# Attention in front of a soft mixture of experts: rotary products, sums and roundings placed earlier, the row of maxima on another queue

## Chip, cores and metric

The kernel runs on one core of a Trainium2 chip. The metric is the device time of one execution in microseconds (us), lower is better. Engines are named as in the profile: PE (matrix products), PEld (its weight loads), DVE (vector), ACT (scalar/activation), POOL (GpSimd) and SP (SyncE, which here only issues DMAs). A "q" behind a name (ACTq, SPq) is that engine's sequencer, for instance while it issues a DMA.

## What is computed

The reference is an attention, a soft mixture of experts on its output, and a gated MLP on that. Only the attention part is touched by the change:

```python
def rotate(x):
    x1, x2 = (x[..., :half], x[..., half:])
    return np.concatenate([x1 * cos - x2 * sin, x1 * sin + x2 * cos], axis=-1)
q_rot, k_rot = (rotate(q), rotate(k))
scores = scale * np.matmul(q_rot, k_rot.transpose(0, 1, 3, 2))
scores = scores - np.max(scores, axis=-1, keepdims=True)
attn = np.exp(scores)
attn = attn / (np.sum(attn, axis=-1, keepdims=True) + 1e-09)
return np.matmul(attn, v)
```

There are 4 batches of 8 heads, 576 positions, head size 64. Then `x` is [2304, 512]; `_moe_ref` (8 experts, 4 slots each, 512 to 1024 to 512) and `_moe2_ref` (512 to 2048 to 512 with `h * sigmoid(h)`) follow.

## The kernel before

**Pairs and groups.** The 32 heads are worked on as 16 pairs `p` of two heads. The attention of one pair is ten groups: two halves `h` of the 576 queries, and in each half five chunks `c` of keys in the order 4, 0, 1, 2, 3, where chunk 4 holds the remaining 64 keys of both heads together. `groups` (160 entries) is the order of PE's main work, and the loop over `g` near the end of the attention code writes everything out by hand: nothing is scheduled by a planner. In each turn it emits `scores` (four matmuls and two exponentials; chunk 4 has four matmuls and one), at most one unit of the row maxima, `esum`, `session`, and then `run(g)`, the list of further tasks that stand under this group's number. Below, "place i" is g modulo 10, so places 0 and 5 are the chunk 4 groups.

**Exponentials.** `scores` makes two products for each tile of scores (L397 and L398, for chunk 4 L386 and L387): one of the rounded keys and queries, and one with 65 rows, of which the last is a row of -1 on the key side and the row of maxima on the query side (row 64 of the tile `qb`). ACT takes the exponential (L399, L388). Three buffers of PSUM (`st`) hold the scores.

**Row maxima.** A pair needs nine units. A unit is two products (L345; the first from `kd`, a difference of two halves of the keys made by `k_diff`, L334), a ReLU on ACT (L350) and a reduction on DVE (L359) that frees the second buffer. Three buffers of PSUM (`mx`) and two of SBUF hold them. `MAX_AT` says at which places of a pair's ten groups one unit is done: in the kernel before, at all but place 4. They serve the pair after next or the next one, since they start at place 6 (`MAX_FROM`). `max_rows` (L367) then transposes the nine columns of maxima on PE, and `max_copy` (L372) copies the result on ACT and issues the DMA into row 64 of `qb` (L373) from ACT's own queue. Both stand under `MAX_ROW`, four groups ahead of the pair's first group, that is at place 6.

**Rotary.** `rotary(p)` gives the steps for pair `p`; queries and keys lie in the tile `raw`, [128, 2 heads, 2, 576]. f0 (L269, DVE) multiplies by the cosine, f1 (L272, POOL) by the sine, f2 (L275, DVE) adds the two, f3 (L279, ACT) rounds the sum, f4 (L284, DVE) takes what the rounding left. Each is done once for each head, f0(0), f0(1) and so on. m0 and m1 (L288) are five DMAs on SP's queue that spread the result into `sa` and `kb`, m2 (L304) another one into `qb`. The tuples `ROT_2`, `ROT_3`, `ROT_4` (pairs 2, 3, 4) and `ROT` (pairs 5 to 15) give, for begin, f0(0), f1(0), f1(1), f0(1), f2(0), f2(1), f3(0), f3(1), m0, f4(0), f4(1), m1 in this order, how many groups ahead of the pair's first group each stands. -22 is thus place 8 of a pair's ten groups, two to three pairs earlier.

**The other tasks.** `load` (L224) fetches `raw` of a pair from HBM, at `QK_LOAD`; there are two buffers. `load_v` (L232) fetches the values. `fetch` (L138), `conv` (L148 on ACT, L151 and L154 on DVE) and `keep` (L647, L648) bring weights of the last stage to 32 bits; `W_IN_AT` places them. `load_w` (L134) prefetches weights of the experts. All of these DMAs are issued by SP, which works through its list in order and waits at each one until its buffer is free. `esum` (L411, L413, L414, L416) sums exponentials on POOL at places 2, 3, 7 and 8. `sums` (L435, L437, at places 2 and 7), `recip` (L440, L444) and `norm`, `norm2` (L448, L449, L455) make the quotient; `x_t` (L467, L471 to L477, at `X_T`) transposes the output; `batch` (`BATCH`) makes the mixture's logits and slots once for four pairs. `sums`, `x_t`, `max_rows` and parts of `batch` share one buffer of PSUM, with the tag `m`.

```python
ROT = (-29, -26, -27, -26, -25, -24, -22, -23, -22, -21, -21, -20, -20)
...
at(g0 + o[min(p, 5) - 2], rt(p, k, *a))
...
at(g0 + (MAX_ROW_1, MAX_ROW_2, MAX_ROW_3, MAX_ROW)[min(p, 4) - 1], lambda p=p: max_rows(p), lambda p=p: max_copy(p))
```

Of the kernel before, what the change touches and what calls it, by code (L numbers as in the profile page):

```python
# [7 lines left out]
F32 = mybir.dt.float32  # L8
# [9 lines left out]
NPAIR = 16  # L18
# [20 lines left out]
ROT_2 = (-26, -22, -19, -21, -23, -19, -19, -18, -18, -18, -17, -18, -17)  # L39
ROT_3 = (-31, -25, -27, -26, -26, -24, -23, -23, -22, -16, -22, -19, -15)  # L40
ROT_4 = (-28, -28, -26, -28, -24, -23, -23, -20, -22, -17, -19, -21, -17)
ROT = (-29, -26, -27, -26, -25, -24, -22, -23, -22, -21, -21, -20, -20)
Q_COPY = -6
V_LOAD = -6
K_DIFF_2 = -14
K_DIFF_3 = -15
K_DIFF_4 = -16
K_DIFF = -17
QK_LOAD = -34
QK_LOAD_3 = -54  # L50
QK_LOAD_4 = -31
MAX_ROW = -4
MAX_ROW_1 = -4
MAX_ROW_2 = -4
MAX_ROW_3 = -5
RECIP = 7
NORM = 7
X_T = ((21, 25), (15, 21), (15, 21), (15, 21))
W_IN_AT = (9, 20, 30, 40, 49, 60, 70, 81, 89, 100, 110, 120)
W_IN_STEPS = (1, 1, 5)  # L60
FETCH_AHEAD = 5
BATCH = (14, 16, 20, 21, 22, 23, 25, 30)
W_LOADS = (34, 54, 64, 75, 66, 84, 86, 76, 105, 95, 116, 135, 126, 144, 127, 134, 135, 136, 144, 155)
SCALES = -19
EARLY = -10
MAX_AT = (1, 1, 1, 1, 0, 1, 1, 1, 1, 1)
MAX_FROM = (6, 2, 6)
MAX_COUNTS = (0, 1, 2, 2, 2, 2, 0, 0, 1, 1, 1, 1, 1, 2, 2, 0, 1, 1, 1, 1, 1, 1, 1, 1, 1, 2, 1, 1, 1, 1, 1, 1, 1, 1, 2, 1, 1, 1, 1, 1)

# [5 lines left out]
def attn_softmoe_mlp_kernel(ctx: ExitStack, tc: tile.TileContext, qk, v, cst, phi, w1, w2, w_in, w_out, out):  # L75
    nc = tc.nc
    pe, act, dve, pool, sp = nc.tensor, nc.scalar, nc.vector, nc.gpsimd, nc.sync
# [113 lines left out]
    with tc.manual_schedule():  # L191
        with ExitStack() as t1:
# [22 lines left out]
            def operands(p):  # L215
                return sa[p % 3] + [qb_[p % 2], kb_[p % 3]]
# [3 lines left out]
            def load(p, heads=None, parts=(slice(0, 2),)):  # L220
                if p not in raw:
                    raw[p] = rw.tile([128, 2, 2, S], F32, tag=f"raw{p % 2}", name=f"raw{p}")
                if heads is None:
                    sp.dma_start(out=raw[p], in_=qk[p])  # L224
                else:
                    for hd in heads:
                        for i in parts:
                            sp.dma_start(out=raw[p][:, hd, i], in_=qk[p, :, hd, i])
# [135 lines left out]
            def max_rows(p):  # L364
                assert mdone[p] == 9
                t = ps_m.tile([128, 512], F32, tag="m", name=f"psm{p}")
                pe.transpose(t[0:9, 0:128], mx.pop(p), ident)  # L367
                mrow[p] = t

            def max_copy(p):  # L370
                m = (p2 if p % 2 else eb).tile([9, 128], F32R, tag="m", bufs=1, name=f"m{p}")
                act.activation(out=m, in_=mrow.pop(p)[0:9, 0:128], func=ACTF.Copy)  # L372
                act.dma_start(out=operands(p)[2][64:65].bitcast(F32), in_=m.bitcast(F32))  # L373

            et = {}
            u_ps = {}
# [82 lines left out]
            def x_t(p, part):  # L459
                b, j = divmod(p, 4)  # L460
                if j == 0 and part == 0:
                    xc[b] = p1.tile([128, 6, DM], F32, tag="x", name=f"x{b}")
                cs = [(c, n) for c, (o, n) in enumerate(CHUNKS[b]) if (o >= HS if b == 3 else c == 4) == part]
                t = ps_m.tile([128, 4, 128], F32, tag="m", name=f"xps{p}_{part}")
                for i, (c, n) in enumerate(cs):
                    o = CHUNKS[b][c][0]
                    pe.transpose(t[0:n, i], xt[p][:, o:o + n], ident)  # L467
                full = sum(n == 128 for c, n in cs)
                c0 = cs[0][0]
                if b == 3:  # L470
                    act.activation(out=xc[b][0:96, c0:c0 + 3, 128 * j:128 * j + 128], in_=t[0:96, 0:3], func=ACTF.Copy)  # L471
                    return
                if full:
                    act.activation(out=xc[b][:, c0:c0 + full, 128 * j:128 * j + 128], in_=t[:, 0:full], func=ACTF.Copy)
                if full < len(cs):
                    c, n = cs[-1]
                    act.activation(out=xc[b][0:n, c, 128 * j:128 * j + 128], in_=t[0:n, full], func=ACTF.Copy)  # L477
# [151 lines left out]
            def at(g, *fs):  # L629
                tasks.setdefault(g, []).extend(fs)  # L630
# [10 lines left out]
            def conv(i):  # L641
                n, k = divmod(i, 4)
                o = wa.tile([128, 512], F32, tag=f"w{NWA - 5 + i % 2}", name=f"w_in_32_{i}")

                def keep():
                    if n == 0:
                        sp.dma_start(out=w_in_0[:, k], in_=o[:, 0:128])  # L647
                    sp.dma_start(out=w_in_32[n][:, k], in_=o if n else o[:, 128:512])  # L648

                cv[i] = (*narrow(words.pop(i), o, wa, f"hw{i}", f"w{NWA - 3}"), keep)  # L650
# [11 lines left out]
            def begin_batch(b):  # L662
                bt[b] = batch(b)

            def bf(b, k, *a):
                return lambda: bt[b][k](*a)

            ROTARY = [([r[i] for r in (ROT_2, ROT_3, ROT_4, ROT)], k, a) for i, (k, a) in enumerate(((8, ()), (0, (0,)), (1, (0,)), (1, (1,)), (0, (1,)), (2, (0,)), (2, (1,)), (3, (0, act)), (3, (1, act)), (5, ()), (4, (0,)), (4, (1,)), (6, ())))]

            for p in range(NPAIR):  # L670
# [8 lines left out]
                if p >= 3:  # L679
                    at(g0 + (QK_LOAD_3, QK_LOAD_4, QK_LOAD)[min(p, 5) - 3], lambda p=p: load(p))  # L680
                if p >= 1:
                    at(g0 + (MAX_ROW_1, MAX_ROW_2, MAX_ROW_3, MAX_ROW)[min(p, 4) - 1], lambda p=p: max_rows(p), lambda p=p: max_copy(p))
                if p == NPAIR - 1:
# [8 lines left out]
                for i in range(2 * (p < NPAIR - 1)):  # L692
                    at(g0 + X_T[p % 4][i], lambda p=p, i=i: x_t(p, i))
                if p % 4 == 3 and p < NPAIR - 1:
                    b = p // 4
                    at(g0 + BATCH[0], lambda b=b: begin_batch(b), bf(b, 0, 0))
                    at(g0 + BATCH[1], bf(b, 0, 1))
                    at(g0 + BATCH[2], bf(b, 1, 0))
                    at(g0 + BATCH[3], bf(b, 1, 1))
                    at(g0 + BATCH[4], bf(b, 2))  # L700
                    at(g0 + BATCH[5], bf(b, 3))
                    at(g0 + BATCH[6], bf(b, 4))
                    at(g0 + BATCH[7], bf(b, 5))
            for i in range(12):
                gc = W_IN_AT[i]
                at(gc, lambda i=i: conv(i), lambda i=i: cv[i][0]())
# [79 lines left out]
            g3(0, act)  # L786
            nk(0)
            max_copy(0)
            h3q(0)
            load(2, (1,))  # L790
# [19 lines left out]
            for g in range(NG + 2):  # L810
                i = g % 10
                if g < NG:
                    p, h, c = groups[g]
                    if i == (MAX_FROM[p] if p < 3 else 6) and p + 2 < NPAIR:
                        ms += [(p + 2, u) for u in range(9)]
                    u = [ms.pop(0) for _ in range(min(len(ms), MAX_COUNTS[g] if g < len(MAX_COUNTS) else MAX_AT[g % 10]))]
                    way = [x[1] % 2 if g < 5 else 0 for x in u]
# [397 lines left out]
```

## Time and profile before

| what | value |
|---|---|
| median of 3 runs | 675.57 us (671.97 to 676.7) |
| the profiled execution's own time | 679.32 us |
| its span, first to last instruction | 677.5 us |
| mean granted TensorE clock | 0.959 of full speed |
| PE busy | 612.3 us, 90% of the span |
| DVE, ACT, POOL busy | 60%, 53%, 34% |

The profile is of one execution. Busy time of PE is modelled from pipelined matmuls, whose durations overlap; the start times tell how fast they follow each other. The attention lasts until about 390 us of the span; behind it come the experts (to about 430 us) and the gated MLP. A row that ends in "[1.54 <-DVE raw L275]" says that the engine stood idle for 1.54 us before this instruction and which instruction ended the wait.

### The profile page before, as it was taken

The page shows a single profiled execution, that of the slowest core. Times are in us where ns is not written, and L with a number is a line of the kernel's source. Part 1 is how long each engine was busy: PE and PEld are TensorE (multiplying, and loading weights), DVE is VectorE, ACT ScalarE, POOL GpSimd, SP SyncE. Part 2 cuts the span into 40 slices and gives each one's busy share as a digit, 9 for nine tenths or more (in the row PEclk, how much of TensorE's full clock was granted, in tenths as well). Part 3 has the DMA queues.
Part 4 walks back from the last instruction along what each step waited for, and adds up shares of the span by engine and source line. Part 5 has one row for each costly group of instructions (what it writes and reads, how often), then busy time and mean ns, then how long its engine had stood idle before and what let it go on. Part 6 is the DMA issues. An engine that isn't in the chain of part 4 may idle for free.

```text
span 677.5 us, 10493 instructions
## 1 busy us (share of the span) xinstructions
PE 612.3 (90%) x3571; PEld 429.9 (63%) x3571; DVE 404.6 (60%) x865; ACT 358.9 (53%) x920; POOL 233.5 (34%) x195
## 2 busy tenths in 40 slices
PE   5678799988989889888999999997989999999997
PEld 2555566565666655665666433375768888888886
DVE  6675487757666786677533523268994544454443
ACT  3455467665756665656565412178764543344442
POOL 5466276646656575558245000002340000000000
PEclk9778799989989999889899989998999999999999
DMA  6885479756877778674886099965330200020002
GB/s 214 203 231 163 147 220 267 210 141 198 273 210 217 244 214 246 150 216 136 245 312 223 1 360 386 399 238 160 120 93 1 94 0 1 0 94 1 0 1 93
DMA packets 43188, 113.86 MB, mean 168 GB/s; under 512 B 4976, under 2 KB 6272, under 8 KB 41344
## 3 DMA queue, kind: packets, MB, share of 16 engines
q1 hardware_dynamic: 42704, 112.80, 53.5%
q8 instruction: 28, 0.46, 0.3%
q10 hardware_dynamic: 432, 0.40, 0.2%
q14 instruction: 24, 0.20, 0.1%
HBM read 78.12 MB, written 7.60 MB: 127 GB/s over the span
## 4 chain that ended last, share of the span: by engine, by line
PE 60%; ACT 14%; issue 9%; DVE 9%; DMA 3%; POOL 2%; ACTq 1%; SPq 1%; DVEq 0%; POOLq 0%
PE ops L1156 8%; PE ops L1157 8%; PE u L426 8%; PE ops L1155 8%; PE psmx L345 4%; ACT e L399 4%; PE st L397 3%; DVE raw L275 3%; PE l L900 3%; ACT relu L350 3%; ACT raw L279 3%; PE l L879 2%; PE st L398 2%; PE u L423 2%; PE s L435 2%
## 5 line engine op out<-in xcount | busy, mean ns | idle before, releaser
L399 ACT ACTIVATE e<-st 128x288 f32<-128x288 f32 x256 | 101.5, 415 | 52.6 <-PE st L398 40.7
L1156 PE MATMUL ops<-wo_lo,ghi 128*128 128x512 f32 x288 | 113.0, 393 | 0.5 <-POOL wo_lo L1033 0.5
L1157 PE MATMUL ops<-wo_hi,glo 128*128 128x512 f32 x288 | 113.0, 392 | 0.0
L1155 PE MATMUL ops<-wo_hi,ghi 128*128 128x512 f32 x288 | 113.0, 393 | 0.0
L359 DVE CUSTOM_DVE_ANT_0 relu<-psmx,relu 128x288 f32<-128x288 f32 x144 | 64.7, 452 | 73.1 <-ACT relu L350 58.7
L1057 DVE TENSOR_TENSOR hps<-hps,g 128x384 f32<-128x384 f32 x96 | 50.0, 561 | 82.1 <-ACT g L1054 81.9
L411 POOL TENSOR_TENSOR es<-e,e 128x576 f32<-128x576 f32 x31 | 44.1, 1424 | 130.4 <-ACT e L399 130.4
L397 PE MATMUL st<-sa,sa 128*128 128x288 f32 x256 | 88.3, 348 | 0.5 <-ACT e L399 0.4
L1054 ACT ACTIVATE g<-hps 128x384 f32<-128x384 f32 x96 | 42.5, 490 | 82.0 <-PE hps L1050 81.7
L426 PE MATMUL u<-e,v 128*64 128x288 f32 x512 | 82.3, 442 | 0.0
L398 PE MATMUL st<-qb,kb 65*128 65x288 f32 x256 | 77.6, 305 | 0.0
L345 PE MATMUL psmx<-sa,sa 128*128 128x288 f32 x160 | 50.0, 331 | 20.9 <-ACT relu L350 17.2
L350 ACT ACTIVATE relu<-psmx 128x288 f32<-128x288 f32 x144 | 59.1, 413 | 12.3 <-PE psmx L345 11.6
L397 PEld LDWEIGHTS st<-sa,sa 128*128 128x128 f32 x256 | 50.5, 197 | 23.7 <-issue 17.3
L272 POOL TENSOR_TENSOR raw<-raw,tab 128x576 f32<-128x576 f32 x31 | 57.3, 1864 | 13.9 <-DMA sa<-sa 8.3
L1157 PEld LDWEIGHTS ops<-wo_hi,glo 128*128 128x128 f32 x288 | 54.5, 189 | 11.8 <-issue 0.2
L1156 PEld LDWEIGHTS ops<-wo_lo,ghi 128*128 128x128 f32 x288 | 54.5, 189 | 10.7 <-POOL wo_lo L1033 0.8
L1155 PEld LDWEIGHTS ops<-wo_hi,ghi 128*128 128x128 f32 x288 | 54.2, 188 | 9.8 <-issue 0.2
L345 PE MATMUL psmx<-kd,sa 128*128 128x288 f32 x160 | 48.5, 319 | 12.1 <-DMA sa<-raw 6.2
L426 PEld LDWEIGHTS u<-e,v 128*64 128x64 f32 x512 | 36.8, 144 | 32.9 <-issue 18.1
L416 POOL TENSOR_TENSOR es<-es,e 128x576 f32<-128x576 f32 x31 | 53.4, 1722 | 5.6 <-ACT e L399 3.5
L269 DVE TENSOR_TENSOR raw<-raw,tab 128x576 f32<-128x576 f32 x32 | 50.8, 1595 | 4.8 <-DMA tab<-in_cst_dram 4.8
(193 smaller groups left out, 1036.7 us busy)
## 6 DMA issues: line engine op xcount, KB each, us to landing
w<-in_w_dram SPq DMA_DIRECT2D x64, 512.0 KB, 9.0
sa<-raw SPq DMA_DIRECT2D x56, 288.0 KB, 4.4
raw<-in_qk_dram SPq DMA_DIRECT2D x13, 1152.0 KB, 8.0
w_out_raw<-in_w_out_dram SPq DMA_DIRECT2D x16, 512.0 KB, 5.8
w_in_raw<-in_w_in_dram SPq DMA_DIRECT2D x12, 512.0 KB, 4.7
v<-in_v_dram SPq DMA_DIRECT2D x15, 320.0 KB, 3.2
qb<-sa SPq DMA_DIRECT2D x16, 288.0 KB, 5.2
out_dram<-os SPq DMA_DIRECT2D x18, 256.0 KB, 2.2
```

The costliest lines, as they stand in the source:

```text
L272: eng.tensor_tensor(out=r[:, hd, 1], in0=r[:, hd, 1], in1=c(1), op=ALU.mult)
L345: pe.matmul(t, lhsT=rem_cols(qa, hd, 128) if u == 4 else qa[:, c0:c0 + 128], rhs=k, start=u != 4 or hd == 0, stop=u != 4 or hd == 1)
L350: act.activation(out=r, in_=t, func=ACTF.Relu)
L359: dve.tensor_tensor_reduce(out=r, in0=mxt.pop((p, u, 1)), in1=r, scale=1.0, scalar=-3.0e38, op0=ALU.add, op1=ALU.max, accum_out=mx[p][:, u ...
L397: pe.matmul(st, lhsT=ka[:, c0:c0 + 128], rhs=qa[:, o:o + HS], start=True, stop=False)
L398: pe.matmul(st, lhsT=kb[0:65, c0:c0 + 128], rhs=qb[0:65, S * hd + HS * h:S * hd + HS * h + HS], start=False, stop=True)
L399: act.activation(out=e[:, hd], in_=st, func=ACTF.Exp, scale=0.125)
L416: add(out=es[p, h], in0=es[p, h], in1=e, op=ALU.add)
L426: pe.matmul(u_ps[p, h][64 * hd:64 * hd + 64, :], lhsT=vt[p][:, c, 64 * hd:64 * hd + 64], rhs=e[:, hd], start=False, stop=c == 3, skip_grou ...
L1155: pe.matmul(t, lhsT=a, rhs=wo_hi[k], start=k == 0, stop=False)
L1156: pe.matmul(t, lhsT=a, rhs=wo_lo[k], start=False, stop=False)
L1157: pe.matmul(t, lhsT=b, rhs=wo_hi[k], start=False, stop=k == 15)
```

## The change

For pairs 5 to 15 the rotary steps move: f0(0) four groups earlier, f1(0) three, f1(1) two, f0(1) one, f2(0) one, f2(1) two, both f4 one; f3, m0 and m1 stay. `load` of those pairs stands one group earlier (place 5), as does the row of maxima for pairs 4 to 15 (place 5). The place without a unit of maxima is 5 in place of 4. The first transposition of the output stands at place 6 in place of 5, and so does the transposition in `batch`; the first of the weight conversions stands one group later. The DMA of the row of maxima is issued from SP's queue for pairs 1 to 14, and from ACT's queue for pairs 0 and 15 as before.

```diff
-ROT = (-29, -26, -27, -26, -25, -24, -22, -23, -22, -21, -21, -20, -20)
+ROT = (-31, -30, -30, -28, -26, -25, -24, -23, -22, -21, -22, -21, -20)
...
-QK_LOAD = -34
+QK_LOAD = -35
...
-MAX_ROW = -4
+MAX_ROW = -5
...
-X_T = ((21, 25), (15, 21), (15, 21), (15, 21))
-W_IN_AT = (9, 20, 30, 40, 49, 60, 70, 81, 89, 100, 110, 120)
+X_T = ((21, 26), (16, 21), (16, 21), (16, 21))
+W_IN_AT = (10, 20, 30, 40, 49, 60, 70, 81, 89, 100, 110, 120)
...
-BATCH = (14, 16, 20, 21, 22, 23, 25, 30)
+BATCH = (14, 16, 20, 21, 22, 23, 26, 30)
...
-MAX_AT = (1, 1, 1, 1, 0, 1, 1, 1, 1, 1)
+MAX_AT = (1, 1, 1, 1, 1, 0, 1, 1, 1, 1)
...
             def max_copy(p):
                 m = (p2 if p % 2 else eb).tile([9, 128], F32R, tag="m", bufs=1, name=f"m{p}")
                 act.activation(out=m, in_=mrow.pop(p)[0:9, 0:128], func=ACTF.Copy)
-                act.dma_start(out=operands(p)[2][64:65].bitcast(F32), in_=m.bitcast(F32))
+                (act if p in (0, NPAIR - 1) else sp).dma_start(out=operands(p)[2][64:65].bitcast(F32), in_=m.bitcast(F32))
```

## Rows read from the trace of the kernel before

**Rows 1.** The page: granted clock of PE, tenths in 40 slices of 16.9 us

```profile
PEclk9778799989989999889899989998999999999999
```

**Rows 2.** Windows by stage: length, busy of PE, PEld, DVE, ACT, POOL, granted clock, DMA

```profile
100.00:325.00 225.00, 202.40 (x1314) 138.37 (x1313) 159.01 (x352) 139.40 (x394) 137.55 (x102) 0.96 0.73 208
325.00:390.00 65.00, 62.73 (x450) 39.63 (x449) 28.69 (x78) 37.84 (x107) 22.33 (x20) 1.00 0.55 194
```

**Rows 3.** What PE waited for, 100 to 325 us: total, times, longest

```profile
PE psmx L345 <- ACT relu L350: 16.1, 11, 1.8
PE st_r L387 <- DMA qb<-m: 2.0, 3, 1.1
PE psm L367 <- DVE lt L512: 1.6, 2, 0.8
PE s L435 <- ACT x L474: 1.0, 2, 0.5
```

**Rows 4.** What ACT waited for, 100 to 325 us

```profile
ACT raw L279 <- DVE raw L275: 16.6, 11, 1.6
```

**Rows 5.** Timeline of ACT in one pair, places 6 to 9: start, length

```profile
224.52 0.74 ACTq L373 DMA_DIRECT2D qb<-m  x1
225.31 0.41 ACT L399 ACTIVATE e<-st 128x288 f32<-128x288 f32 x1 [0.82 <-PE psmx L345]
...
227.96 0.40 ACT L350 ACTIVATE relu<-psmx 128x288 f32<-128x288 f32 x1
...
230.20 0.69 ACT L279 ACTIVATE raw<-raw 128x576 fp32r<-128x576 f32 x1 [1.54 <-DVE raw L275]
```

**Rows 6.** Timeline of DVE in the same pair, places 8 to 0

```profile
228.66 0.45 DVE L359 CUSTOM_DVE_ANT_0 relu<-psmx,relu 128x288 f32<-128x288 f32 x1
...
229.03 1.14 DVE L275 TENSOR_TENSOR raw<-raw 128x576 f32<-128x576 f32 x1
...
233.37 0.75 DVE L284 TENSOR_TENSOR raw<-raw 128x576 f32<-128x576 f32 x1
```

**Rows 7.** Timeline of PE at place 0 of another pair, and its next sums

```profile
278.64 2.19 PE L426 MATMUL u<-e,v 128*64 128x288 f32 x8
...
283.91 1.16 PE L426 MATMUL u<-e,v 128*64 128x288 f32 x8
```

**Rows 8.** Windows at half clock: the first and the last of six

```profile
144.70:148.10 3.40, 3.40 (x14) 2.27 (x11) 2.06 (x5) 0.98 (x3) 0.00 (x0) 0.51 0.99 219
...
322.20:325.60 3.40, 3.40 (x14) 2.02 (x11) 0.87 (x3) 0.47 (x2) 0.00 (x0) 0.50 0.98 213
```

**Rows 9.** The tile `raw`: shortest, median and longest ns of its steps

```profile
L269 DVE TENSOR_TENSOR raw<-raw,tab x32: 745/1774/1979, 5.7 to 311.1; 128x576 f32<-128x576 f32 x32
L284 DVE TENSOR_TENSOR raw<-raw x32: 751/753/1618, 8.7 to 322.3; 128x576 f32<-128x576 f32 x32
```

**Rows 10.** POOL's instructions by line, 100 to 325 us

```profile
L416 POOL TENSOR_TENSOR es<-es,e 128x576 f32<-128x576 f32 x21 | 38.6, 1836 | 1.6
L272 POOL TENSOR_TENSOR raw<-raw,tab 128x576 f32<-128x576 f32 x20 | 38.2, 1927 | 0.0
```

**Rows 11.** What DVE waited for, 100 to 325 us

```profile
DVE relu L359 <- ACT relu L350: 35.7, 32, 2.9
```

**Rows 12.** Timeline of SP's queue, places 3 to 5 of a pair

```profile
239.56 1.11 SPq L138 DMA_DIRECT2D w_in_raw<-in_w_in_dram  x1
240.72 0.51 SPq L134 DMA_DIRECT2D w<-in_w_dram  x1
241.33 0.38 SPq L224 DMA_DIRECT2D raw<-in_qk_dram  x1
```

**Rows 13.** Timeline of PE around the row of maxima of that pair

```profile
241.75 1.19 PE L426 MATMUL u<-e,v 128*64 128x288 f32 x8
...
245.44 0.27 PE L367 MATMUL psm<-cst_sb,mx 128*9 128x128 f32 x1 [0.82 <-DVE lt L512]
```

**Rows 14.** The page's DMA issues: count, KB each, median us from issue to landing

```profile
raw<-in_qk_dram SPq DMA_DIRECT2D x13, 1152.0 KB, 8.0
```

## Prediction

> **What bounds the kernel now.** I read the page first: in the first half of its slices PE's granted clock is not always full [rows 1]. The table by stage says where there is room. From 325 us on PE is busy nearly without a break in the attention's tail. Between 100 and 325 us, where pairs 5 to 15 pass through their rotary steps, PE is busy for 202.4 of 225 us at a mean clock of 0.96, and no other engine is above 71% (DVE, 159.0 of 225) [rows 2]. So PE's idle time in that stretch is to be explained, and the waits do it. 16.1 us stand at one place: the second product of a unit of maxima waits for a ReLU of ACT, 11 times, at most 1.8 us. Another 2.0 us, in three waits, is for the DMA of the row of maxima; the rest is near 3 us [rows 3]. Eleven is the number of pairs 5 to 15.
>
> ACT's waits say why the ReLU is late. ACT waits 11 times, 16.6 us in all, in the rounding f3 for the sum f2 [rows 4]. The timelines of one pair show the loop. ACT issues the row's DMA for 0.74 us, and the next exponential begins 0.82 us late though its scores were there. Then it runs without a gap up to f3(1) at place 8 and stands for 1.54 us [rows 5]. DVE could not start f2(1) earlier: the sum stands in the same group, behind that group's reduction, which itself waits for ACT's ReLU that ended at 228.36; f2(1) runs from 229.03 for 1.14 us [rows 5, 6]. So ACT waits for DVE, which waited for ACT, once a pair. PE runs ahead until its buffers for the maxima are full and then stands for up to 1.8 us [rows 3].
>
> The stall has a second price. Right behind six of the eleven the granted clock is at the lower of its two levels (1.2 GHz of 2.4) for a window of 3.4 us, in which PE is busy throughout [rows 8]; eight instructions of the values' product take 2.19 us there and 1.16 us soon after [rows 7]. At half clock 3.4 us do the work of 1.7 us: up to 1.7 us lost in each, 10.2 us for six.
>
> **The change part by part.**
>
> *Sums and roundings.* f2(0) to f3(0) and f2(1) to f3(1) now have two groups between them. f3(1) at place 8 finds a sum from place 6, where DVE no longer depends on the ReLU of place 8. A group lasts about 2 us (ten fill a pair's 21 to 22 us), so the sum is about 4 us ahead and its 1.14 us fit. ACT's 1.5 us a pair go, and with the 0.82 us below ACT reaches place 0 some 2.3 us sooner, more than the longest stall of PE (1.8). Gain: 16.1 us of PE's waits at most, and with the stalls the 10.2 us of half clock. At least nothing, if another engine is as late there.
>
> *Products.* f0(0) leaves place 4, where it stood right behind `kd` (place 3), for place 0; f0(1) moves from 5 to 4 and f1 to places 0 and 2 on POOL. Their number is unchanged. f0 takes 0.75 to 1.98 us, the long ones beside POOL [rows 9]. DVE's crowd at places 3 to 6 loses one f0 and gains f2(1), the shorter one; places 8 to 0 get f0(0) and both f4. On POOL f1(1) now stands between the two halves of a sum of exponentials, which ends 1.9 us later [rows 10]; it is needed five groups, some 10 us, after its start and takes about 6.7 us with f1(1), so it stays hidden. If that cover went, PE would wait at `sums`.
>
> *The two f4.* They take 0.75 us now, on a DVE without POOL beside it [rows 9]. One group earlier they fall beside the sums of exponentials, of which one instruction takes 1.84 us [rows 10]. The bounds are 0.75 us and 0.75 + 1.84 = 2.6 us; the nearest row is f4's own longest, 1.62 us, so I take 1.6: 1.7 us more DVE time a pair for the two. In this stretch DVE idles for ACT's ReLU 35.7 us in all [rows 11], and PE has a long product of values at place 0, so I cost it at 0.3 us of PE a pair at most. Here the Trainium skill speaks against the change: "SBUF — State Buffer", section "Who interferes with whom", says that a DVE instruction with two SBUF inputs and a GpSimd instruction that reads SBUF exclude each other for the whole instruction. f0's spread agrees with it [rows 9]. By the rule the two f4 could cost DVE up to the 2.6 us each above; that case is the first rival.
>
> *Row of maxima.* ACT is rid of 0.74 us of issue, 11 times in the stretch, on a path where ACT was late; this is part of the 2.3 us above and not added again. The row leaves one group earlier, ahead of the load of `raw` in SP's queue, so I expect PE's 2.0 us for it to go [rows 3]; bounds 0 and 2.0.
>
> *What waits behind it.* SP now stands at the row until ACT has copied it. Behind it in the queue are the load of `raw`, the fetch of weights, an expert's weights and the next m0. At present SP runs ahead: `raw` was issued at 241.33 us [rows 12], and the row's transposition ran only at 245.44 [rows 13]. One place earlier, and without its 0.82 us behind `batch`, the transposition can run when the values' product of place 5 ends, at 242.9 [rows 13]. With the copy and SP's issue `raw` then goes out at about 244, 2.7 us later than now. It lands 8.0 us after its issue at present [rows 14], with a fetch of weights and an expert's weights issued just ahead of it [rows 12]; most of those will have landed by then, and the fetch stands behind it, so I take 6 us; 8.0 is the upper bound. Its reader, f0(0), comes four groups earlier than now, about where f4(1) of place 0 ran. In the pair of [rows 5, 6] that was 233.37, and about 232 with PE's stall gone. `raw` would go out there at about 224 and land between 230 and 232. So it just arrives, and f0(0) may be up to 1.5 us late before the next reduction holds PE, because PE has the values' product of place 0 in hand. I take 0 and keep the case as a rival.
>
> The Trainium skill, "DMA: Bandwidth & Descriptors", section "Anatomy of one DMA — SWDGE (gpsimd) path", says that a wait happens on the issuing sequencer and the DMA engines never wait; that is why the row's wait holds everything behind it on SP. The order on SP's queue in this trace agrees [rows 12].
>
> *Transposition of the output* moves behind the row on the shared buffer, just ahead of `sums` at place 7. PE waited twice for ACT's copy ahead of `sums`, 1.0 us in all [rows 3]. If each of 11 pairs pays such a half microsecond it is 5 us; I take a few tenths, 2 us in all. The batch's copies, 1.6 us in two waits [rows 3], change place and keep their price. The place without a unit, and the weights' first conversion, I cost at nothing: the same count of instructions, in groups where PE or ACT has slack.
>
> **Sum.** 16.1 + 10.2 + 2.0 = 28.3 us can go. Back come about 2 us at the transpositions and 2.3 us of stalls left at place 0 (0.2 a pair). 28.3 - 4.3 = 24 us, 3.5%. The profiled execution took 679.32 us around a span of 677.5; it would be 655.3. It lies 3.75 us above the median of 675.57, so on the median I forecast 651.6 us.
>
> **The rivals.**
>
> *The stall only shrinks.* What waits at place 0 is then DVE: two f4 of up to 2.6 us and f0(0) of 2.0 us in three groups. For it speaks that DVE is the second busiest engine (71%) and that POOL works just then; against it that DVE idled for ACT's ReLU there [rows 11]. If 1 us a pair comes back, with half of the low clock windows, the gain is 28.3 - 11 - 5 = 12 us: about 664.
>
> *SP's queue decides: slower.* `raw` waits behind the row, f0(0) and f1(0) wait for `raw`, and DVE's reductions wait behind f0(0), so PE's buffers stay full. Up to 1.5 us is covered; beyond that the wait adds itself and, by [rows 8], up to 1.7 us of low clock. At a wait of X the pair pays X - 1.5 + 1.7 against 2.57 gained (28.3 over 11), so it decides from X = 2.4 us. With the load landing 11 us after its issue X is about 3: 3.2 times 11 is 35.2, less 28.3, slower by 7: about 682. Against it: at most one load is left ahead of `raw`.
>
> *The step does not do what it says.* f3(1) is not the cause but ACT's own load is; its wait moves to another instruction of ACT and PE's eleven stalls remain. Then only the row's 2.0 us go: 673.6. Against it: ACT is busy for 139 of 225 us [rows 2].
>
> **How the numbers follow.** Forecast (646 to 658) 0.72; the stall only shrinks (658 to 668) 0.16; no change (669 to 682) 0.06; slower 0.06. The median of before may move by some 0.5%, and about 1% is what a measurement of this kernel can tell from no change. The low end is all 28.3 us and 2 us of runs' spread, 645; the high end takes in most of the second case, 666. Faster by over 1%: 0.72 + 0.16, so 0.88; within 1% 0.06; slower 0.06.
>
> **What would show it.** Right: ACT's waits for f2 in f3 fall from 16.6 us to under 2, PE's eleven waits for the ReLU to under 4 us, the granted clock between 100 us and the end of the rotary steps is above 0.98, and POOL and DVE show no wait for `raw`. Wrong: a new wait of DVE's f0 or POOL's f1 for the load of `raw`, or PE's wait at the maxima put down to a DVE reduction, or low clock windows that stay without the stall.

## The result

The changed kernel takes 646.45 us (median of 4 runs, 645.01 to 647.71), the kernel before 676.13 us in the same session: ratio 0.9556, 95% interval 0.9484 to 0.9627. Run once more beside other kernels it took 645.88 us, ratio 0.9572 (0.9526 to 0.9617). The profiled execution took 647.71 us around a span of 645.8.

To set like against like, the windows below run from the start of pair 2's first `sums` on PE to the start of pair 12's second, the same work in each kernel. The columns are those of [rows 2]; first the kernel before, then the changed one.

```profile
96.65:327.45 230.80, 208.20 (x1353) 142.85 (x1352) 161.60 (x361) 144.58 (x409) 139.85 (x104) 0.96 0.72 207
```

```profile
92.91:294.34 201.43, 195.22 (x1352) 139.13 (x1351) 166.58 (x358) 145.78 (x409) 139.67 (x104) 1.00 0.87 243
```

29.4 of the 31.7 us by which the spans differ lie in this stretch. PE is now busy for 97% of it at full clock. Ahead of the stretch the two profiles differ by 3.7 us. The change reaches little of that part (the rows of pairs 1 and 2, the load and the first products of pair 5, the first weights' conversion), and the kernel with the two sums alone, which is unchanged there, differs from the kernel before by 2.3 us; so I make nothing of it. Behind the stretch the changed kernel's profile is 1.4 us longer.

The page's clock line of the changed kernel, in slices of 16.1 us, answers to [rows 1]:

```profile
PEclk9679899999999999999989999989999999999999
```

What PE waited for between 95 and 305 us of the changed kernel, to be read against [rows 3]:

```profile
PE xps L467 <- ACT x L477: 1.3, 2, 0.7
PE psm L367 <- DVE mx L359: 1.3, 4, 0.7
PE s L435 <- DVE lt L512: 1.0, 2, 0.5
PE s L435 <- ACT x L474: 1.0, 2, 0.5
PE st L397 <- ACT e L399: 0.5, 1, 0.5
```

The eleven waits for the ReLU and the three for the row are not there any more. On ACT the wait in f3 [rows 4] is gone too; what it waits for is PE, and three times a load of weights:

```profile
ACT m L372 <- PE psm L367: 15.1, 11, 2.2
ACT rs L440 <- PE s L437: 12.5, 21, 1.2
...
ACT hw L148 <- DMA w_in_raw<-in_w_in_dram: 4.9, 3, 2.3
```

The timelines of one pair show the order that does it, first DVE, then ACT, then POOL (start, length). They answer to [rows 5, 6].

```profile
149.95 0.74 DVE L275 TENSOR_TENSOR raw<-raw 128x576 f32<-128x576 f32 x1
...
152.41 0.47 DVE L448 SCALAR_TENSOR_TENSOR s<-s,r 128x288 f32<-128x288 f32 x1 [1.34 <-ACT r L444]
...
154.22 1.88 DVE L284 TENSOR_TENSOR raw<-raw 128x576 f32<-128x576 f32 x1
```

```profile
153.49 0.42 ACT L399 ACTIVATE e<-st 128x288 f32<-128x288 f32 x1
153.78 0.69 ACT L279 ACTIVATE raw<-raw 128x576 fp32r<-128x576 f32 x1
154.35 0.42 ACT L399 ACTIVATE e<-st 128x288 f32<-128x288 f32 x1
```

```profile
154.06 1.42 POOL L416 TENSOR_TENSOR es<-es,e 128x576 f32<-128x576 f32 x1 [0.36 <-ACT e L399]
```

f2(1) is over at 150.7, ahead of `norm` (L448), which still waits 1.34 us for ACT. f3(1) follows ACT's exponential without a gap. f4 at 154.22 took 1.88 us beside POOL.

### The profile page after: what moved, and what is told of

The parts are those of the page before. It is cut to its first block, busy times and chain, and to the rows that moved or that the text cites. A ratio compares the mean times of both kernels' runs of the same rounds, so it can differ in the third digit from the quotient of the medians.

```text
span 645.8 us, 10527 instructions
## 1 busy us (share of the span) xinstructions
PE 597.1 (92%) x3571; PEld 425.1 (66%) x3571; DVE 410.1 (63%) x865; ACT 360.6 (56%) x920; POOL 234.0 (36%) x195
## 4 chain that ended last, share of the span: by engine, by line
PE 69%; ACT 12%; DVE 9%; DMA 5%; issue 3%; POOL 0%; ACTq 0%; DVEq 0%; SPq 0%; POOLq 0%
PE ops L1155 9%; PE ops L1157 9%; PE ops L1156 9%; PE u L426 8%; PE psmx L345 5%; PE st L397 4%; PE l L900 3%; PE st L398 3%; PE s L435 3%; ACT e L399 3%; PE s L437 2%; PE hps L1050 2%; PE l L879 2%; PE u L423 2%; ACT raw L279 2%
## 5 line engine op out<-in xcount | busy, mean ns | idle before, releaser
L399 ACT ACTIVATE e<-st 128x288 f32<-128x288 f32 x256 | 104.2, 419 | 28.3 <-PE st L398 25.7
L397 PE MATMUL st<-sa,sa 128*128 128x288 f32 x256 | 86.2, 338 | 0.5 <-ACT e L399 0.5
L411 POOL TENSOR_TENSOR es<-e,e 128x576 f32<-128x576 f32 x31 | 46.2, 1491 | 95.9 <-ACT e L399 95.9
L426 PE MATMUL u<-e,v 128*64 128x288 f32 x512 | 78.2, 422 | 0.0
L272 POOL TENSOR_TENSOR raw<-raw,tab 128x576 f32<-128x576 f32 x31 | 55.5, 1795 | 16.2 <-DMA sa<-sa 8.2
L1156 PEld LDWEIGHTS ops<-wo_lo,ghi 128*128 128x128 f32 x288 | 54.3, 189 | 10.2 <-POOL wo_lo L1033 0.4
L345 PE MATMUL psmx<-sa,sa 128*128 128x288 f32 x160 | 48.5, 320 | 8.0 <-DVE mx L359 6.4
L1063 DVE TENSOR_TENSOR glo<-hps,ghi 128x384 fp32r<-128x384 f32 x96 | 49.6, 552 | 5.3 <-ACT ghi L1060 2.0
```

The lines of the kernel that those rows point to most:

```text
L272: eng.tensor_tensor(out=r[:, hd, 1], in0=r[:, hd, 1], in1=c(1), op=ALU.mult)
L345: pe.matmul(t, lhsT=rem_cols(qa, hd, 128) if u == 4 else qa[:, c0:c0 + 128], rhs=k, start=u != 4 or hd == 0, stop=u != 4 or hd == 1)
L397: pe.matmul(st, lhsT=ka[:, c0:c0 + 128], rhs=qa[:, o:o + HS], start=True, stop=False)
L399: act.activation(out=e[:, hd], in_=st, func=ACTF.Exp, scale=0.125)
L426: pe.matmul(u_ps[p, h][64 * hd:64 * hd + 64, :], lhsT=vt[p][:, c, 64 * hd:64 * hd + 64], rhs=e[:, hd], start=False, stop=c == 3, skip_grou ...
L1156: pe.matmul(t, lhsT=a, rhs=wo_lo[k], start=False, stop=False)
```

## The experiments

Each kernel differs from the one named by the lines shown. Each ratio is to the kernel before in the same session; the table's runs come from three, in which that kernel's medians were 673.7, 676.3 and 680.4 us. The stretch is the one above, pair 2's first `sums` to pair 12's second, from each run's profile; the clock is PE's mean granted clock in it, as a share of full speed.

| kernel | median us | ratio to before, 95% | stretch us | clock |
|---|---|---|---|---|
| changed, run again | 645.88 | 0.9572 (0.9526 to 0.9617) | 201.02 | 1.00 |
| ROT alone | 650.5 | 0.9687 (0.9646 to 0.9728) | 205.83 | 1.00 |
| two sums alone | 652.3 | 0.9659 (0.9618 to 0.9700) | 206.74 | 1.00 |
| queue alone | 677.15 | 1.0062 (1.0003 to 1.0121) | 228.41 | 0.97 |
| changed, row on ACT | 650.2 | 0.9679 (0.9652 to 0.9706) | 205.26 | 1.00 |
| changed, sums back | 668.75 | 0.9931 (0.9898 to 0.9964) | 222.95 | 0.98 |
| changed, sum behind norm | 655.71 | 0.9661 (0.9596 to 0.9726) | 210.55 | 1.00 |
| changed, same group, ahead of norm | 650.14 | 0.9580 (0.9516 to 0.9643) | 205.39 | 1.00 |
| changed, f3(1) written four times | 686.03 | 1.0160 (1.0114 to 1.0205) | 239.85 | 0.93 |
| changed, rows 1 and 2 on ACT | 647.11 | 0.9582 (0.9535 to 0.9628) | 204.45 | 0.99 |
| changed, row 15 on SP | 646.69 | 0.9512 (0.9439 to 0.9586) | 202.11 | 1.00 |
| changed, fetch one group earlier | 648.37 | 0.9560 (0.9493 to 0.9627) | 201.18 | 1.00 |

The changed kernel itself stood beside the first of them:

> The changed kernel once more, as the base for the three beside it: 643 to 649 us, ratio to the kernel before 0.950 to 0.963.

### The rotary steps alone, and the queue alone

```diff
-ROT = (-29, -26, -27, -26, -25, -24, -22, -23, -22, -21, -21, -20, -20)
+ROT = (-31, -30, -30, -28, -26, -25, -24, -23, -22, -21, -22, -21, -20)
```

> The kernel before with the new tuple ROT alone; row of maxima on ACT's queue at place 6, everything else as before. Theory A (ACT stood in f3 for a sum of its own group, and that made PE's eleven stalls and the low clock): ACT's wait in f3 falls from 16.6 us to under 2, PE's wait for the ReLU from 16.1 to about 3, no low clock window behind it; the row's 2.0 us of waits stay. 676 - 13 - 10 = 653 us (650 to 657), PE's waits of the early pairs as before. Theory B (the row on ACT's queue was the larger half of ACT's lateness): PE's stall stays at 0.8 us or more a pair, 662 us or above.

```diff
-                act.dma_start(out=operands(p)[2][64:65].bitcast(F32), in_=m.bitcast(F32))
+                (act if p in (0, NPAIR - 1) else sp).dma_start(out=operands(p)[2][64:65].bitcast(F32), in_=m.bitcast(F32))
```

> The kernel before with only the queue of the row's DMA changed (pairs 1 to 14 on SP). Theory A: ACT comes 0.8 us sooner through places 6 to 8, DVE's sum with it, so the wait in f3 stays at 1.5 us and PE's stall shrinks from 1.5 to about 0.7 us: 9 us, the row's 2.0 us, and some of the low clock windows (5 us): 660 us (655 to 668). Theory B (queue is the larger half): below 655. Theory C (SP held at the row delays the load of raw and the fetch): 675 or above, with waits of DVE, POOL or ACT for those loads.

ROT alone, in the kernel before, takes the stretch from 230.80 to 205.83 us: 25.0 of the 29.4. The queue alone gains nothing in the median. In its profile the row's 2.0 us of waits are gone and four windows at the lower clock stand in place of six, but PE's stall is 5.7 us longer. Its waits of ACT and of PE, 95 to 325 us:

```profile
ACT raw L279 <- DVE raw L275: 19.5, 11, 2.4
```

```profile
PE psmx L345 <- ACT relu L350: 21.8, 11, 2.6
```

ACT came sooner, as expected, and then waited longer in f3: 19.5 us in place of 16.6 [rows 4]. My theory had DVE's sum come sooner with it. It did not, and the timelines of this kernel, first ACT, then DVE, show why:

```profile
204.47 0.50 ACT L440 ACTIVATE rs<-s,eps 128x288 f32<-128x288 f32 x1 [0.50 <-PE s L437]
```

```profile
205.47 0.47 DVE L448 SCALAR_TENSOR_TENSOR s<-s,r 128x288 f32<-128x288 f32 x1 [0.24 <-ACT r L444]
...
207.28 1.21 DVE L275 TENSOR_TENSOR raw<-raw 128x576 f32<-128x576 f32 x1
```

f2(1) stands behind `norm`, which waits for ACT's quotient, which here waits 0.50 us for PE's `sums`. So ACT's earlier arrival does not bring `norm` forward by as much. In the two pairs of the kernel before that I looked at, ACT began the quotient 0.1 and 0.4 us behind the (modelled) end of the `sums`, so there was no more than that to gain.

### The queue and the sums, undone in the changed kernel

```diff
-                (act if p in (0, NPAIR - 1) else sp).dma_start(out=operands(p)[2][64:65].bitcast(F32), in_=m.bitcast(F32))
+                act.dma_start(out=operands(p)[2][64:65].bitcast(F32), in_=m.bitcast(F32))
```

> The changed kernel with the row's DMA back on ACT's queue for all pairs; the rest as changed. Theory A: PE bounds the stretch now and ACT waits there for PE, so 0.74 us of issue a pair is hidden or costs up to 0.3 us of PE a pair; the early pairs lose PE's 3.9 us of waits for the row behind SP's loads: 643 to 650 us. Theory B (queue is the larger half): PE's stall at the maxima returns, 655 us or above.

```diff
-ROT = (-31, -30, -30, -28, -26, -25, -24, -23, -22, -21, -22, -21, -20)
+ROT = (-31, -30, -30, -28, -26, -24, -22, -23, -22, -21, -22, -21, -20)
```

> The changed kernel with f2(0) and f2(1) back at -24 and -22 in ROT, f3 and all else as changed: one and no group between sum and rounding. Theory A: ACT waits in f3(1) for about 1.5 us a pair again; it starts 0.8 us sooner than in the kernel before, so PE stalls for some 0.7 to 0.9 us a pair, with a part of the low clock windows: 656 us (652 to 662). Rival (the products and their place on DVE did it, not the distance of sum and rounding): within 1% of the changed kernel, 642 to 651, and no wait in f3.

With the sums ahead, the queue is worth some 4 us (205.26 to 201.02 in the stretch; the intervals of the two ratios do not overlap). With the row on ACT PE waits longer for ACT's copies of the transposed output, 5.4 us in place of the 2.3 above:

```profile
PE xps L467 <- ACT x L477: 3.0, 2, 1.5
PE s L435 <- ACT x L474: 2.4, 5, 0.5
```

Without the sums ahead the queue is worth about nothing. The kernel with the row on ACT also stands for what was not taken apart: it differs from ROT alone by the row's place, the load of `raw`, the transpositions, the weights' first conversion and the place without a unit. Together these bring 0.6 us of stretch, and the two ratios can't be told apart.

The sums back in their old groups cost 22 us of stretch; I had expected about 10. ACT's wait in f3 is back at 17.6 us in 11 times, so ACT kept none of the 0.8 us by which it starts sooner:

```profile
ACT raw L279 <- DVE raw L275: 17.6, 11, 2.2
```

```profile
PE psmx L345 <- ACT relu L350: 19.9, 11, 2.4
```

### The sums alone

```diff
-ROT = (-29, -26, -27, -26, -25, -24, -22, -23, -22, -21, -21, -20, -20)
+ROT = (-29, -26, -27, -26, -25, -25, -24, -23, -22, -21, -21, -20, -20)
```

> The kernel before with only the two sums moved in ROT: f2(0) one group earlier, f2(1) two, so that f2(1) stands ahead of norm on DVE. Theory A (f2(1) stood on DVE behind norm, which waits for PE's sums and ACT's quotient; taken ahead of it the wait in f3 goes): ACT's wait in f3 under 3 us in all, PE's eleven stalls under 5 us, 650 to 656 us. Rival (with both f0 still at places 4 and 5 DVE's crowd there is too late for it, and the products had to move as well): the wait in f3 stays above 8 us or PE waits for DVE's reductions instead, 660 us or above.

Two numbers of the tuple bring 24.1 of the 29.4 us. No wait for the ReLU is left. DVE's crowd at places 4 to 6 shows, but costs little:

```profile
PE psmx L345 <- DVE mx L359: 2.6, 4, 0.8
```

So the products did not have to move; with them (ROT alone) the stretch is 0.9 us shorter, and the two ratios can't be told apart.

### Distance, or the order against `norm`

The first kernel puts f2(1) one group later, where the list has it behind `norm`. The second has it in the same group, but first in the list.

```diff
-ROT = (-31, -30, -30, -28, -26, -25, -24, -23, -22, -21, -22, -21, -20)
+ROT = (-31, -30, -30, -28, -26, -25, -23, -23, -22, -21, -22, -21, -20)
```

> The changed kernel with f2(1) at -23 in place of -24: one group between sum and rounding, and f2(1) now behind norm of place 7 on DVE. Theory A (norm decides: its three instructions wait for PE's sums and ACT's quotient, and what stands behind them comes too late for f3(1)): ACT waits in f3(1) again, 0.7 to 1.5 us a pair, PE's stall at the maxima returns: 654 to 668 us. Rival (any distance of one group is enough): within 1% of the changed kernel, 640 to 652, no wait in f3.

```diff
-ROT = (-31, -30, -30, -28, -26, -25, -24, -23, -22, -21, -22, -21, -20)
+ROT = (-31, -30, -30, -28, -26, -25, -23, -23, -22, -21, -22, -21, -20)
...
-                        at(g0 + o[min(p, 5) - 2], rt(p, k, *a))
+                        (first if p >= 5 and (k, a) == (2, (1,)) else lambda g, f: at(g, f))(g0 + o[min(p, 5) - 2], rt(p, k, *a))
```

> The same as the one before, f2(1) in the same group at -23, but put first in that group's list, ahead of norm on DVE; nothing else differs. Theory A (norm decides): no wait in f3, 643 to 650 us, as the changed kernel. Rival (the number of groups between decides): the same time as with f2(1) behind norm.

Behind `norm` ACT waits in f3(1) in each of the eleven pairs, 0.8 us in the mean, and PE behind it; here ACT's waits and then PE's of that kernel:

```profile
ACT raw L279 <- DVE raw L275: 9.0, 11, 0.9
```

```profile
PE psmx L345 <- ACT relu L350: 4.5, 11, 0.4
PE psmx L345 <- DVE mx L359: 3.9, 11, 0.4
```

Ahead of it, in the same group, no wait in f3 is left in the stretch. It is 5.2 us shorter (205.39 against 210.55). The intervals of the two ratios overlap, but the four times of either kernel, taken in one session, do not (648.85 to 652.59 us against 654.26 to 658.00). It does not reach the changed kernel's 201.02: DVE's reductions come later there, and PE waits for them 2.9 us at the row's transposition, in place of 1.3, and 1.9 us at the maxima, in place of none. f2 takes 1.97 us in the median of that stretch, against 0.75 in the changed kernel. So the order against `norm` decides whether ACT waits at all. Distance has its share: with the sums back, where f2(1) stands one more group later, ACT's wait is 17.6 us, and with f2(1) in this group but behind `norm` it is 9.0.

### ACT's time by itself

f3(1) is written three more times with the same values, for pairs 5 to 15.

```diff
-                        at(g0 + o[min(p, 5) - 2], rt(p, k, *a))
+                        at(g0 + o[min(p, 5) - 2], *[rt(p, k, *a)] * (4 if p >= 5 and (k, a) == (3, (1, act)) else 1))
```

> The changed kernel with f3(1) written three more times in its place (same values) for pairs 5 to 15: 3 x 0.58 = 1.7 us of pure ACT time a pair at place 8, about the wait that the change took away, with no wait for DVE. Theory A (what stalls PE at place 0 is ACT's lateness, whatever makes it): PE waits for the ReLU again, 0.5 to 1.0 us a pair, some low clock windows: 652 to 662 us. Rival (ACT has slack there and only the wait for DVE's sum mattered): 645 to 650.

It costs 38.8 us of stretch (239.85 against 201.02), where I had expected 10 or so. The four take 2.85 us where one takes 0.69, so it is 2.2 us more a pair and not the 1.7 of my expectation. ACT's busy time in the stretch rose by 22.8 us, and the cost is 1.7 times that. The windows of the changed kernel, run again, and of this one (columns as in [rows 2]):

```profile
95.11:296.13 201.02, 195.09 (x1353) 138.98 (x1352) 166.78 (x358) 145.63 (x409) 139.77 (x104) 1.00 0.86 243
```

```profile
95.59:335.44 239.85, 210.57 (x1352) 144.58 (x1351) 155.47 (x358) 168.45 (x442) 135.10 (x104) 0.93 0.72 205
```

The four f3 of one pair, PE's waits in the stretch, PE at place 0 of that pair and a window there:

```profile
210.34 2.85 ACT L279 ACTIVATE raw<-raw 128x576 fp32r<-128x576 f32 x4
```

```profile
PE psmx L345 <- ACT relu L350: 24.7, 11, 2.2
```

```profile
213.84 0.60 PE L345 MATMUL psmx<-sa,sa 128*128 128x288 f32 x2 [2.25 <-ACT relu L350]
```

```profile
214.20:217.60 3.40, 3.40 (x13) 1.29 (x12) 1.80 (x6) 0.48 (x2) 0.00 (x0) 0.50 1.01 280
```

There are eleven stalls, and behind ten of them a window of 3.4 us at the lower clock: 24.7 + 10 x 1.7 = 41.7 us, 2.9 more than the measured cost. Taken from the windows instead, PE's idle time rose by 23.4 us and its busy time by 15.5. So both prices that the prediction added up, the stall and the clock, are there in a kernel that has only ACT's lateness, and their sum is some 7% too high.

### Three attempts to go further

```diff
-                (act if p in (0, NPAIR - 1) else sp).dma_start(out=operands(p)[2][64:65].bitcast(F32), in_=m.bitcast(F32))
+                (act if p in (0, 1, 2, NPAIR - 1) else sp).dma_start(out=operands(p)[2][64:65].bitcast(F32), in_=m.bitcast(F32))
```

> The changed kernel with the row's DMA of pairs 1 and 2 on ACT's queue, as before the change; the others on SP. In the profile PE waited 0.85 and 3.0 us for these two rows behind SP's bulk loads, with 6.8 us of low clock behind the second. Theory A: those waits go, 2 to 4 us faster than the changed kernel (642 to 645). Rival: the early pairs are held by other waits (DVE, SP's transfers), which take them over: within 1 us of it.

```diff
-                (act if p in (0, NPAIR - 1) else sp).dma_start(out=operands(p)[2][64:65].bitcast(F32), in_=m.bitcast(F32))
+                (act if p == 0 else sp).dma_start(out=operands(p)[2][64:65].bitcast(F32), in_=m.bitcast(F32))
```

> The changed kernel with the row of pair 15 on SP's queue as well. In the changed kernel its issue took ACT 1.31 us, and PE then waited 1.47 us for ACT's copy of the transposed output, with a low clock window of 3.4 us. Theory A: these go, 2 to 3 us faster than the changed kernel (643). Rival: SP stands there at the prefetch of weights, so the row comes late, PE waits for it: 648 or above.

```diff
-FETCH_AHEAD = 5
+FETCH_AHEAD = 6
```

> The changed kernel with the fetch of weights one group earlier, mostly ahead of the row on SP's queue in place of behind it. In the changed kernel ACT waited three times, 4.9 us, for those weights. Theory A (SP held at the row delays what is behind it, but ACT's wait at place 0 is hidden behind PE's product of values): ACT's waits for the weights go and the time stays within 2 us of the changed kernel (644 to 648). Rival (the fetch ahead of the load of raw makes that load late for f0): DVE or POOL wait for raw, 650 or above.

None can be told from the changed kernel (ratios 0.9582, 0.9512 and 0.9560, with intervals that hold 0.9572). With the rows of pairs 1 and 2 on ACT, PE still waited 1.8 us for the second one, in place of 3.9 us for the two. The stretch of that profile is 3 us longer: ACT waited 4.2 us for one load of weights, PE 2.4 us for ACT, and a window at the lower clock stands behind it. With pair 15 on SP, PE's wait at the tail's transposition fell from 1.5 to 0.6 us, which the medians do not show. The window behind that wait is gone as well, but the changed kernel, run again, has none there either. With the fetch ahead of the row ACT's 4.9 us of waits for weights go and the stretch stays at 201.18: they were hidden, but for one wait of PE for ACT of 0.5 us.

## Why the prediction was right, and where its steps failed

**Right: what bounds, and the two prices.** The stall of PE behind f3 was 16.1 us and its clock 10.2; both went to nothing in the stretch, with the row's 2.0: 28.3 us against 29.4 measured there. The ACT time put back bears both out. The measured 646.45 us lies 0.45 us inside the range's low end, so the number is right by little.

**Wrong: what f2(1) waited for.** I had it "behind that group's reduction, which itself waits for ACT's ReLU". In [rows 6] that reduction, at 228.66, stands without a wait. Ahead of it DVE had waited for ACT's quotient, and then worked through `norm` and `norm2`:

```profile
227.22 0.47 DVE L448 SCALAR_TENSOR_TENSOR s<-s,r 128x288 f32<-128x288 f32 x1 [0.51 <-ACT r L444]
...
228.28 0.46 DVE L455 SCALAR_TENSOR_TENSOR xt<-u,rs 128x288 f32<-128x288 f32 x1
```

The reduction was only the last in line. Ahead of it but behind `norm` about half of ACT's wait stays (9.0 us); ahead of `norm` none does. That the two groups of the change carry f2(1) past `norm` as well was luck: the prediction does not name `norm`, and with one group less the kernel takes 655.71 us. Hence the step "with the 0.82 us below ACT reaches place 0 some 2.3 us sooner" was wrong as two gains that add up: 0.82 us off ACT, alone, turned into more waiting in f3. It counts only once the sum is ahead, and then for about 4 us.

**Mis-sized: what comes back.** I took 4.3 us, 2 of them at the transpositions and 2.3 at stalls left at place 0. Of the stalls nothing is left. The other waits of PE come to 5.1 us in the rows above, against 3.8 before (2.6 in the last two of [rows 3] and two smaller ones, 0.7 and 0.5; "near 3 us" was a misreading): 1.3 us more where I had put 4.3. That is the larger reason why 24 us was too little. The other is PE's (modelled) busy time, which fell by 13.0 us in the stretch where I had 10.2. With the two sums alone, at full clock, it fell by 10.7 (208.20 to 197.53); what took off the other 2.3 us is not shown. In the tail PE's wait for ACT's copy rose from 0.6 to 1.5 us; with pair 15's row on SP it is 0.6 again.

**Held: the products at no cost**, on a DVE that is busy for 83% of the stretch now (70% before). **The f4** were put at 1.6 us each; the rows of `raw` (shortest, median and longest, as [rows 9]) say 1.3 in the median, and f2, moved away from POOL, fell to 0.75, from a median of 1.14 in the stretch before:

```profile
L284 DVE TENSOR_TENSOR raw<-raw x32: 748/1310/1875, 8.8 to 290.6; 128x576 f32<-128x576 f32 x32
...
L275 DVE TENSOR_TENSOR raw<-raw x30: 739/748/1983, 7.3 to 283.4; 128x576 f32<-128x576 f32 x30
```

So one pair of instructions left POOL's company and the other came into it. The rule of the Trainium skill ("SBUF — State Buffer", section "Who interferes with whom") fits both rows. The first rival did not come: PE waits for no reduction at the maxima in the stretch.

**SP's queue.** The rival's mechanism is there, its price is small. SP's queue waits at the row in every pair of the stretch (its waits, 95 to 305 us):

```profile
SPq L373 <- ACT relu L350: 49.6, 11, 5.5
SPq L288 <- PE st L397: 32.5, 11, 4.3
```

What SP waits at the row it mostly does not wait at m0, which stood for 86.9 us between 100 and 325 us in the kernel before. POOL waited once, 1.0 us, in f1:

```profile
POOL raw L272 <- DMA w<-in_w_dram: 1.0, 1, 1.0
```

The profile names an expert's weights, which were issued next but one behind `raw`; f1 reads `raw`, so I take it for that load. DVE waited for no load. What the Trainium skill says ("DMA: Bandwidth & Descriptors", section "Anatomy of one DMA — SWDGE (gpsimd) path"), that a semaphore wait happens on the issuing sequencer, fits SP's rows. PE's 2.0 us for the row are gone in the stretch, as forecast. Ahead of it PE waits 3.9 us for the rows of pairs 1 and 2, where it waited 0.3 before, and 6.8 us at the lower clock begin there (74.9 us); the prediction had no term for that.

## What to carry to other kernels

On an engine that does its list in order, as DVE here, look at what an instruction stands behind: moved ahead of a step that waits for two other engines, the sum needed no more distance for ACT to stop waiting. Time taken off an engine counts only if that engine's next wait does not end at a time that others set; here the same 0.74 us a pair was worth nothing alone and about 4 us in all with the sum ahead. When PE stands behind another engine again and again, add to its wait what the low clock behind it costs.

## What was not expected

A stall of PE can cost nearly twice its length. In the kernel before eleven stalls of 0.45 to 1.76 us had six windows of 3.4 us at 1.2 GHz behind them. With f3(1) written four times ten of eleven stalls, 2.2 us each, had one. But with the sums back only three of eleven stalls of 1.3 to 2.4 us had one, and with the queue alone four of eleven of 1.4 to 2.6 us. So a stall's length alone does not tell: one of 2.46 us had no window behind it, one of 1.65 us had; what decides is not shown here. With the sum behind `norm`, at most 0.9 us a pair, there is none, and the stretch is longer by 9.5 us for 8.4 us of PE's waits at the maxima. So 2.2 us more of ACT's time a pair, in a stretch where ACT is busy for 72%, made a kernel that is 4% faster than the one before into one that is 1.6% slower.
